# A planner's durations for two engines set to measured ones, with three smaller edits, in a kernel that chains a convolution and two expert layers

## The chip, the cores and the metric

The kernel runs on one core of one Trainium2 chip. The metric is device time in microseconds (us) of one execution, the median over runs. The core's engines are TensorE (PE in the profile; PEld is its weight load), VectorE (DVE), ScalarE (ACT), GpSimd (POOL) and SyncE (SP), which here only issues DMAs. Each engine takes its instructions in the order in which the program lists them and waits at the head of its queue for what an instruction needs.

## The reference

`x` is 2 x 4096 x 192, `weight_gen` 2 x 4096 x 8 x 7, each expert layer has `w_in` 192 x 2048 and `w_out` 2048 x 192, all float32.

```python
w = softmax(weight_gen, over the 7 taps)
y[b, s, h, :] = sum_k w[b, s, h, k] * x_pad[b, s + k, h, :]     # causal, 6 zero rows in front
x1 = y.reshape(8192, 192)
h = relu(x1 @ moe_w_in);   x2 = (h * h) @ moe_w_out              # layer 0
h = x2 @ moe2_w_in;        out = (h * cos(h)) @ moe2_w_out       # layer 1
```

## The kernel before, in words

The 8192 tokens are 16 blocks `b` of 512. A *step* is one block, one layer `m` and one of 16 slices `f` of 128 hidden units; a *phase* is the 16 steps of one block in one layer. The order of phases is written out: layer 0 of blocks 0 to 5 first, then in turn layer 1 of block b - 6 and layer 0 of block b, at the end layer 1 of the last six blocks. There are 32 phases and 512 steps.

Products keep float32's accuracy by splitting: each operand is the sum of a rounded `hi` and a remainder `lo` of the type fp32r. A step has five matmuls (L608) into one of four PSUM buffers `h`, then `between` (L636) makes the activation, and five matmuls (L625 to L631) add it into `acc`. `between` has for layer 0 a Relu on ScalarE (L642) and a square on ScalarE (L646) or VectorE (L648); for layer 1 `kk` on ScalarE (L652), `rr` on VectorE (L655), Abs and Sin on ScalarE (L657, L658) and the product `g` on VectorE (L660). Then come `hi`, a copy on ScalarE (L275), and `lo = g - hi` (L282). In the first six phases `g` lies in PSUM, and `lo` can only be VectorE's. Afterwards `g` is one of two SBUF buffers, and `lo` may go to VectorE or to GpSimd. The inputs of a layer are split in the same way (`xhi`, `xlo`).

The convolution of a block (`attend`, L470) is four products of `x` with the softmax weights on GpSimd (L460), each cut into `PIECES` parts by heads, each followed by a reduction over the taps on VectorE (L475) that frees one of two buffers `pr`. Transposes and a trip through DRAM turn its result into the input of layer 0. The softmax of later blocks has its last part on VectorE (L421 to L428). The weights of both layers are made from the float32 bits by a chain on ScalarE, VectorE and GpSimd (`weight`, L285: L316 to L333, then L275 and L282).

The order of the instructions on every engine comes from a planner, the class `Order` (L58). Each operation is handed to it with `ways`, the engines that may do it and a duration for each, from the formulas `act`, `dve` and `pool` (L175 to L184). `issue` (L119) first gives each operation a due time: TensorE's follow each other by their durations, and an operation that others depend on is due as much earlier as the shortest of its user's durations, a wait of 0.14 us and the operation's own `ahead` make. It then goes forward in planned time. Of the engines an operation may use it takes the one with the earliest end, where `MORE` adds a handicap to an engine's end in this comparison. Operations with `alone` on VectorE or GpSimd also hold a common `port`, so that in planned time they never overlap:

```python
shared = lambda o, e: o.alone and e in ("dve", "pool")
...
    ((max(free.get(e, 0.0), o.at, free.get("port", 0.0) if shared(o, e) else 0.0) + c, e)
     for e, c in o.ways.items()),
    key=lambda v: v[0] + self.MORE.get(v[1], 0.0))
```

Of the operations that can begin first, the one with the earliest due time is issued. On the chip nothing is left of planned times: only the choice of engine and the order on each engine. At the end `take_out` (L687) stores a block's result with four DMAs from `oa` and two from `ob` (L697), all issued by SyncE.

Of the kernel before, what the change touches and what calls it, by code (L numbers as in the profile page):

```python
# [18 lines left out]
P = 128  # L19
# [5 lines left out]
START = 18.0  # L25
LEAD = 6
AHEAD = 2.0
PIECES = 4
ALONE = 8
WARM = 26  # L30

# [10 lines left out]
class Buf:  # L42
    def __init__(self, make, older=None, before=None, tile=None):
        self.make, self.older, self.before, self.tile = make, older, before, tile
        self.log = []
# [12 lines left out]
class Order:  # L58
# [1 line left out]

    SENT, RATE, SEEN = 0.75, 300e3, 0.8

    MORE = {"dve": 0.6, "pool": 0.0, "act": 0.05}
    NEAR = 0.02
    HALF = 0.15
    BEHIND = 4.0

    def __init__(self):
        self.ops, self.tags, self.since = [], {}, 0.0

    def buf(self, pool, shape, dtype, tag, n, name):
        old = self.tags.setdefault(tag, [])
        b = Buf(
            lambda: pool.tile(shape, dtype, tag=tag, bufs=n, name=name),
            old[-n] if len(old) >= n else None, old[-1] if old else None,
        )
        old.append(b)
        return b
# [14 lines left out]
    def op(self, ways, fn, reads=(), writes=(), size=0, behind=None, by=1e9, over=(), since=0.0,  # L93
           alone=True, slack=0.0, ahead=0.0):
        o = Op()
        o.ways, o.fn, o.size = ways, fn, size
        o.alone, o.slack, o.ahead = alone, slack, ahead
        o.late = self.SENT + size / self.RATE + self.SEEN if size else 0.0
        o.behind, o.by, o.since = behind, by, max(since, self.since)
        o.older, o.deps, o.after, o.n = set(over), set(), set(behind or ()), len(self.ops)  # L100
        for write, accesses in ((False, reads), (True, writes)):
            for a in accesses:
                b, key = a if isinstance(a, tuple) else (a, None)
                for p, w, k in b.log:
                    if (w or write) and (k is None or key is None or k == key):
                        o.deps.add(p)
                if b.log:
                    o.after.add(b.log[0][0])
                elif b.before is not None:
                    o.after.add(b.before.log[0][0])  # L110
                if b.older is not None:
                    o.older.add(b.older)
                b.log.append((o, write, key))
        o.deps.discard(o)
        o.after.discard(o)
        self.ops.append(o)
        return o

    def issue(self):  # L119
# [25 lines left out]
        while ready:  # L145
            for o in ready:
                o.end, o.eng = min(
# [3 lines that stand above are left out]
                o.begin = o.end - o.ways[o.eng]  # L151
# [27 lines left out]
def dve(n, fast=False, psum=False):  # L179
    return 0.147 + n / 960 if psum else 0.069 + n / (1600 if fast else 900)  # L180


def pool(n, scalar=False):
    return 0.08 + n * 0.0011 if scalar else 0.155 + n * 0.0017  # L184


@with_exitstack
def conv_moe_kernel(
# [10 lines left out]
    nc = tc.nc  # L199
# [8 lines left out]
    NB = NT // N  # L208
# [15 lines left out]
    dram = ctx.enter_context(tc.tile_pool(name="dram", bufs=1, space=bass.MemoryType.DRAM))  # L224
    order = Order()
    op, buf = order.op, order.buf
    eng = {"act": nc.scalar, "dve": nc.vector, "pool": nc.gpsimd, "sp": nc.sync, "pe": nc.tensor}

    def sbuf(shape, dtype, tag, n, name):
        return buf(sb, shape, dtype, tag, n, name)  # L230
# [4 lines left out]
    def load(dst, out_fn, in_ap, size, key=None, reads=(), by=1e9, queue="sp", behind=None, slack=0.0):  # L235
        op({queue: 0.45}, lambda e: eng[e].dma_start(out=out_fn(), in_=in_ap), reads=reads,
           writes=[(dst, key)], size=size, by=by, behind=behind, slack=slack)
# [47 lines left out]
    def weight(m, part, c0, n):  # L285
        name = f"{part}{m}_{c0}"
        by = -99.0 if m == c0 == 0 and part != "o" else 1e9

        early = dict(queue="act", behind=exps[:1], by=by) if by < 0 else {}
        if m == 0:  # L290
            order.since = 0.0 if by < 0 else 6.5
        stage = lambda tag, n, shape: (
            order.lent(room[tag], tag + "0", f"{tag}{name}") if m == 0 else sbuf(shape, U32, tag, n, f"{tag}{name}"))
        raw = stage("raw", 2, [P, WC, 2])
# [11 lines left out]
        else:  # L306
# [7 lines left out]


        op({"act": act(cols)}, lambda e: nc.scalar.activation(  # L316
            gt().bitcast(F32), top().bitcast(F32), AF.Abs, scale=2.0 ** -112), [raw], [g])

        def lower(e):
            if e == "act":  # L320
                nc.scalar.activation(vt(), low(), AF.Identity, scale=2.0 ** -29)
            else:
                nc.gpsimd.tensor_scalar(
                    out=vt(), in0=low(), scalar1=2.0 ** -29, scalar2=0.0, op0=ALU.mult, op1=ALU.add)
        op({"act": act(cols), "pool": pool(cols, True)}, lower, [raw], [v])
        op({"dve": dve(cols, True)}, lambda e: nc.vector.tensor_scalar(
            out=st(), in0=top(), scalar1=0x80000000, scalar2=None, op0=ALU.bitwise_and), [raw], [sg])
        op({"dve": dve(cols, True), "pool": pool(cols, True)}, lambda e: eng[e].tensor_scalar(
            out=gt().bitcast(F32), in0=gt().bitcast(F32), scalar1=bits(0x0FEFFFFF), scalar2=0.0,
            op0=ALU.min, op1=ALU.max), [], [g])  # L330
# [24 lines left out]
        for i, (bh, hi, bl, lo, src, size) in enumerate(pieces):  # L355
            if part == "b":
# [2 lines left out]
               [sg], [(bh, (f, "hi", i)) for f in fs], over=over)  # L359
            op({"pool": pool(size), "dve": dve(size)}, lambda e, bh=bh, bl=bl, hi=hi, lo=lo, src=src: sub(e, lo(bl.t), src(), hi(bh.t).bitcast(F32)),  # L360
               [sg] + [(bh, (f, "hi", i)) for f in fs], [(bl, (f, "lo", i)) for f in fs], over=over)
        order.since = 0.0

    def weight_order(m):
        cuts = [0] + list(range(2 * P, DFF, WC)) + [DFF]
# [87 lines left out]
    def product(b, i, pr, inner=False, ways=None):  # L453
        step = H if ways else H // PIECES
        for h0 in range(0, H, step):
            hs = slice(h0, h0 + step)

            def go(e, hs=hs):
                t = pr.t.rearrange("p d k -> p k d") if inner else pr.t
                eng[e].tensor_tensor(  # L460
                    out=t.rearrange("p k (h g) -> p k h g", h=H)[:, :, hs],
                    in0=xc[b].t[:, i:i + K, :].rearrange("p k (h g) -> p k h g", h=H)[:, :, hs],
                    in1=wg[b // CB].t[:, b % CB * BS + i, hs].rearrange("p h k -> p k h").unsqueeze(3).to_broadcast(
                        [P, K, step, G]),
                    op=ALU.mult,
                )
            op(ways or {"pool": pool(K * D * step // H)}, go, [xc[b], (wg[b // CB], b % CB)],
               [pr if step == H else (pr, h0)])
# [201 lines left out]
    def sum_halves(s, o1):  # L670
        op({"act": act(N, True)}, lambda e: copy(e, s.t[DB:P], o1.t[DB:P]), [o1], [s])
        op({"dve": dve(N, psum=True)}, lambda e: nc.vector.tensor_tensor(
            out=s.t[0:DB], in0=o1.t[0:DB], in1=s.t[DB:P], op=ALU.add), [o1], [s], alone=False)
# [13 lines left out]
    def take_out(b):  # L687
        o0, o1 = acc.pop((1, b))
        oa = sbuf([P, N], F32, "raw", 2, f"oa{b}")
        ob = sbuf([DB, N], F32, "raw", 2, f"ob{b}")  # L690
        s = sbuf([P, N], F32, "sum", 1, f"os{b}")
        op({"dve": dve(N)}, lambda e: nc.vector.transpose(oa.t, o0.t), [o0], [oa], alone=False)
        sum_halves(s, o1)
        op({"dve": dve(N)}, lambda e: nc.vector.transpose(ob.t, s.t[0:DB]), [s], [ob], alone=False)
        for d0 in range(0, D, 32):
            o, p0 = (oa, d0) if d0 < P else (ob, d0 - P)
            op({"sp": 0.5}, lambda e, o=o, p0=p0, d0=d0: nc.sync.dma_start(  # L697
                out=out[b * N:(b + 1) * N, d0:d0 + 32].rearrange("(j a) d -> a j d", a=32),
                in_=o.t[p0:p0 + 32].rearrange("a (j d) -> a j d", d=32)), [o], [], size=32 * N * 4)

# [6 lines left out]
    for b in range(NB):  # L707
# [10 lines left out]
        if b % CB == 0:  # L718
# [4 lines left out]
            else:  # L723
                n = 14 + 9 * c
# [13 lines left out]
    def late_weight(t, *w):  # L738
        order.since = 2.27 * t + START - 5
        weight(*w)  # L740
        order.since = 0.0

    for t, w in plan:
        if w[0] == 0:
            when(max(math.floor(t), -1), weight, *w)
        else:
            when(math.floor(t), late_weight, t, *w)
# [59 lines left out]
```

## Time and profile before

| | |
|---|---|
| median of 3 runs | 1265.58 us (1265.26 to 1265.69) |
| the profiled execution | 1267.42 us, its span 1265.5 us |
| mean granted TensorE clock | 0.992 |
| busy share of the span | TensorE 96%, ScalarE 84%, GpSimd 71%, VectorE 50% |
| instructions | 16848 |

The span runs from the first to the last instruction of one profiled execution; the few microseconds beside it are the start and end of the program. The busy share of TensorE is modelled from pipelined matmuls. Shares are means over stages with different limits.

### The profile page before, as it was taken

The page shows a single profiled execution, that of the slowest core. Times are in us where ns is not written, and L with a number is a line of the kernel's source. Part 1 is how long each engine was busy: PE and PEld are TensorE (multiplying, and loading weights), DVE is VectorE, ACT ScalarE, POOL GpSimd, SP SyncE. Part 2 cuts the span into 40 slices and gives each one's busy share as a digit, 9 for nine tenths or more (in the row PEclk, how much of TensorE's full clock was granted, in tenths as well). Part 3 has the DMA queues.
Part 4 walks back from the last instruction along what each step waited for, and adds up shares of the span by engine and source line. Part 5 has one row for each costly group of instructions (what it writes and reads, how often), then busy time and mean ns, then how long its engine had stood idle before and what let it go on. Part 6 is the DMA issues. An engine that isn't in the chain of part 4 may idle for free. (4 is left out here: it accounts for less than half of the span.)

```text
span 1265.5 us, 16848 instructions
## 1 busy us (share of the span) xinstructions
PE 1217.9 (96%) x5344; PEld 987.0 (78%) x5344; DVE 636.8 (50%) x916; ACT 1059.9 (84%) x2003; POOL 893.7 (71%) x879
## 2 busy tenths in 40 slices
PE   7999999999999999999999999999999999999997
PEld 6877878788778787787877877778687878888885
DVE  7667777656271453705416163261723315666654
ACT  4888888788796887969779697887978879999996
POOL 3787887938677596876967768687665665666654
PEclk8999999999999999999999999999999999999999
DMA  5405544202212021121201212011110200111001
GB/s 183 125 32 157 153 142 132 78 22 53 57 38 57 21 75 23 40 55 38 72 9 38 57 38 65 9 38 27 45 26 23 49 21 13 30 30 30 13 4 22
DMA packets 90746, 67.81 MB, mean 54 GB/s; under 512 B 55840, under 2 KB 76320, under 8 KB 90656
## 3 DMA queue, kind: packets, MB, share of 16 engines
q1 hardware_dynamic: 90224, 66.21, 19.2%
q8 instruction: 42, 0.69, 0.2%
q10 hardware_dynamic: 432, 0.52, 0.2%
q14 instruction: 48, 0.39, 0.1%
HBM read 47.24 MB, written 19.46 MB: 53 GB/s over the span
## 5 line engine op out<-in xcount | busy, mean ns | idle before, releaser
L282 POOL TENSOR_TENSOR lo<-g,hi 128x512 fp32r<-128x512 f32 x416 | 538.6, 1298 | 296.7 <-ACT hi L275 207.9
L655 DVE SCALAR_TENSOR_TENSOR rr<-kk,h 128x512 f32<-128x512 int32 x256 | 174.0, 683 | 320.9 <-ACT kk L652 319.0
L275 ACT ACTIVATE hi<-g 128x512 fp32r<-128x512 f32 x416 | 259.4, 623 | 5.9 <-DVE g L660 5.3
L660 DVE TENSOR_TENSOR g<-h,rr 128x512 f32<-128x512 f32 x256 | 175.4, 685 | 100.8 <-POOL lo L282 68.4
L626 PE MATMUL acc<-hi,wo 128*128 128x512 f32 x512 | 200.3, 391 | 1.8 <-POOL wo L282 1.8
L625 PE MATMUL acc<-hi,wo 128*128 128x512 f32 x512 | 200.2, 391 | 1.2 <-ACT hi L275 0.7
L630 PE MATMUL acc<-lo,wo 128*128 128x512 f32 x512 | 200.4, 391 | 0.5 <-POOL lo L282 0.4
L627 PE MATMUL acc<-hi,wo 128*128 128x512 f32 x512 | 200.0, 391 | 0.0
L631 PE MATMUL acc<-lo,wo 128*128 128x512 f32 x512 | 200.0, 391 | 0.0
L646 ACT ACTIVATE g<-rr 128x512 f32<-128x512 f32 x160 | 101.2, 633 | 106.3 <-POOL lo L282 104.0
L657 ACT ACTIVATE rr<-rr 128x512 f32<-128x512 f32 x256 | 160.3, 628 | 26.0 <-DVE rr L655 25.4
L642 ACT ACTIVATE rr<-h 128x512 f32<-128x512 f32 x256 | 149.7, 586 | 23.9 <-PE h L608 23.3
L658 ACT ACTIVATE rr<-rr 128x512 f32<-128x512 f32 x256 | 160.8, 630 | 1.8
L460 POOL TENSOR_TENSOR pr<-xc,wgen_late 128x336 f32<-128x336 f32 x192 | 156.0, 871 | 6.8 <-DVE wgen_late L428 5.0
L652 ACT ACTIVATE kk<-h 128x512 int32<-128x512 f32 x256 | 150.5, 588 | 0.9 <-PE h L608 0.7
L626 PEld LDWEIGHTS acc<-hi,wo 128*128 128x128 f32 x512 | 96.4, 188 | 23.1 <-POOL wo L282 2.7
L630 PEld LDWEIGHTS acc<-lo,wo 128*128 128x128 f32 x512 | 96.4, 188 | 22.2 <-POOL lo L282 2.1
L625 PEld LDWEIGHTS acc<-hi,wo 128*128 128x128 f32 x512 | 96.3, 188 | 22.2 <-ACT hi L275 1.1
L631 PEld LDWEIGHTS acc<-lo,wo 128*128 128x128 f32 x512 | 96.5, 188 | 19.9
L627 PEld LDWEIGHTS acc<-hi,wo 128*128 128x128 f32 x512 | 96.5, 188 | 19.9
L475 DVE TENSOR_REDUCE at<-pr 128x192 f32<-128x1344 f32 x56 | 86.5, 1544 | 30.8 <-POOL pr L460 30.3
L282 DVE TENSOR_TENSOR lo<-h,hi 128x512 fp32r<-128x512 f32 x96 | 65.6, 687 | 50.9 <-ACT hi L275 50.2
(547 smaller groups left out, 2180.1 us busy)
## 6 DMA issues: line engine op xcount, KB each, us to landing
xc<-in_x_dram SPq DMA_DIRECT2D x14, 960.0 KB, 6.1
x2d<-x2a SPq DMA_DIRECT2D x16, 256.0 KB, 2.1
x<-x2d SPq DMA_DIRECT2D x32, 128.0 KB, 2.6
x<-x2d SPq DMA_DIRECT2D x16, 256.0 KB, 2.7
out_dram<-oa SPq DMA_DIRECT2D x64, 64.0 KB, 2.0
x1d<-xt SPq DMA_DIRECT2D x56, 64.0 KB, 1.8
x<-x1d SPq DMA_DIRECT2D x14, 256.0 KB, 2.7
x<-x1d SPq DMA_DIRECT2D x28, 128.0 KB, 5.2
```

The lines of the kernel that those rows point to most:

```text
L275: nc.scalar.activation(out, in_, AF.Copy)
L282: eng[e].tensor_tensor(out=out, in0=in0, in1=in1, op=ALU.subtract)
L460: eng[e].tensor_tensor(out=t.rearrange("p k (h g) -> p k h g", h=H)[:, :, hs], in0=xc[b].t[:, i:i + K, :].rearrange("p k (h g) -> p k h g" ...
L625: nc.tensor.matmul(o0.t, lhsT=w(0), rhs=hi.t, start=start, stop=False)
L626: nc.tensor.matmul(o1.t, lhsT=w(2), rhs=hi.t, start=start, stop=False)
L627: nc.tensor.matmul(o0.t, lhsT=w(1), rhs=hi.t, start=False, stop=False)
L630: nc.tensor.matmul(o1.t, lhsT=w(2), rhs=lo.t, start=False, stop=stop)
L631: nc.tensor.matmul(o0.t, lhsT=w(0), rhs=lo.t, start=False, stop=stop)
L655: op({"dve": dve(N, psum=True)}, lambda e: nc.vector.scalar_tensor_tensor(out=r.t, in0=k.t, scalar=-TWO_PI, in1=h.t, op0=ALU.mult, op1=ALU ...
L657: op({"act": act(N)}, lambda e: nc.scalar.activation(r.t, r.t, AF.Abs), [], [r])
L658: op({"act": act(N)}, lambda e: nc.scalar.activation(r.t, r.t, AF.Sin, scale=-1.0, bias=math.pi / 2), [], [r], behind=exps if (b, f) == (0 ...
L660: op({"dve": dve(N, psum=True)}, lambda e: nc.vector.tensor_tensor(out=g.t, in0=h.t, in1=r.t, op=ALU.mult), [h, r], [g], alone=False)
```

## The change

- `PIECES` goes from 4 to 2: a product on GpSimd is two instructions of 672 elements a partition in place of four of 336.
- `pool(n)`, the duration of a GpSimd instruction with two tensors, becomes 0.13 + n * 0.0023 us in place of 0.155 + n * 0.0017; with a scalar its constant is 0.1 in place of 0.08. The handicap of VectorE in the choice of engine goes from 0.6 to 0.4 us.
- `Order` has a default `ahead`, which `weight` sets to 2.0 us for the loads and the chain of the first weights of layer 0 (parts a and b from column 0), so that each of them is due that much earlier.
- The two stores of `ob` of the last block are issued by ScalarE in place of SyncE.

```diff
-PIECES = 4
+PIECES = 2
...
-    MORE = {"dve": 0.6, "pool": 0.0, "act": 0.05}
+    MORE = {"dve": 0.4, "pool": 0.0, "act": 0.05}
...
-        self.ops, self.tags, self.since = [], {}, 0.0
+        self.ops, self.tags, self.since, self.ahead = [], {}, 0.0, 0.0
...
-        o.alone, o.slack, o.ahead = alone, slack, ahead
+        o.alone, o.slack, o.ahead = alone, slack, max(ahead, self.ahead)
...
 def pool(n, scalar=False):
-    return 0.08 + n * 0.0011 if scalar else 0.155 + n * 0.0017
+    return 0.1 + n * 0.0011 if scalar else 0.13 + n * 0.0023
...
         if m == 0:
             order.since = 0.0 if by < 0 else 6.5
+            order.ahead = 2.0 if by < 0 else 0.0
...
-        order.since = 0.0
+        order.since = order.ahead = 0.0
...
-            op({"sp": 0.5}, lambda e, o=o, p0=p0, d0=d0: nc.sync.dma_start(
+
+            queue = "act" if b == NB - 1 and d0 >= P else "sp"
+            op({queue: 0.5}, lambda e, o=o, p0=p0, d0=d0: eng[e].dma_start(
```

## Rows read from the trace of the kernel before

**Rows 1.** Windows: stretch, length, busy (count) of PE, PEld, DVE, ACT, POOL, clock, DMA.

```profile
263.02:335.54 72.52, 72.52 (x322) 60.08 (x320) 39.19 (x50) 60.35 (x112) 51.00 (x47) 1.00 0.18 48
335.54:376.28 40.74, 38.53 (x162) 31.02 (x160) 23.72 (x33) 37.34 (x72) 28.25 (x26) 0.96 0.13 37
376.28:412.78 36.50, 36.50 (x161) 29.96 (x160) 6.91 (x10) 26.59 (x49) 28.59 (x28) 1.00 0.19 49
335.54:1104.20 768.66, 743.00 (x3201) 599.10 (x3200) 319.79 (x444) 645.95 (x1208) 549.08 (x482) 1.00 0.15 38
1104.20:1249.00 144.80, 144.80 (x634) 118.32 (x633) 89.68 (x140) 138.75 (x265) 89.51 (x70) 1.00 0.10 19
```

**Rows 2.** Waits of the whole span: who waited for whom, us, times, longest.

```profile
ACT g L646 <- POOL lo L282: 104.0, 138, 1.3
...
PEld h L608 <- DVE g L660: 46.9, 55, 2.7
```

**Rows 3.** Timeline of GpSimd and ScalarE, end of a layer 0 phase; start, duration.

```profile
409.98 1.29 POOL L282 TENSOR_TENSOR lo<-g,hi 128x512 fp32r<-128x512 f32 x1 [1.32 <-ACT hi L275]
412.59 1.28 POOL L282 TENSOR_TENSOR lo<-g,hi 128x512 fp32r<-128x512 f32 x1 [1.32 <-PE acc L627]
...
411.30 0.63 ACT L646 ACTIVATE g<-rr 128x512 f32<-128x512 f32 x1 [0.97 <-POOL lo L282]
411.84 0.62 ACT L275 ACTIVATE hi<-g 128x512 fp32r<-128x512 f32 x1
```

**Rows 4.** Groups by line, shapes apart; count, busy us, mean ns, idle before.

```profile
L282 POOL TENSOR_TENSOR lo<-g,hi 128x512 fp32r<-128x512 f32 x416 | 538.6, 1298 | 296.7 <-ACT hi L275 207.9 <-PE h L608 27.0 <-PE acc L627 26.6
...
L660 DVE TENSOR_TENSOR g<-h,rr 128x512 f32<-128x512 f32 x256 | 175.4, 685 | 100.8 <-POOL lo L282 68.4 <-ACT rr L658 19.3 <-ACT rr L642 8.8
L655 DVE SCALAR_TENSOR_TENSOR rr<-kk,h 128x512 f32<-128x512 int32 x256 | 174.0, 683 | 320.9 <-ACT kk L652 319.0
L658 ACT ACTIVATE rr<-rr 128x512 f32<-128x512 f32 x256 | 160.8, 630 | 1.8
...
L460 POOL TENSOR_TENSOR pr<-xc,wgen_late 128x336 f32<-128x336 f32 x192 | 156.0, 871 | 6.8 <-DVE wgen_late L428 5.0 <-DVE at L475 1.3 <-PE acc L627 0.5
L652 ACT ACTIVATE kk<-h 128x512 int32<-128x512 f32 x256 | 150.5, 588 | 0.9 <-PE h L608 0.7
...
L282 DVE TENSOR_TENSOR lo<-h,hi 128x512 fp32r<-128x512 f32 x96 | 65.6, 687 | 50.9 <-ACT hi L275 50.2
```

**Rows 5.** Timeline: a VectorE instruction twice, GpSimd beside it (first, last of five).

```profile
82.24 0.20 DVE L425 TENSOR_SCALAR sx<-sx 128x64 f32<-128x64 f32 x1
...
319.90 4.30 DVE L425 TENSOR_SCALAR sx<-sx 128x64 f32<-128x64 f32 x1
...
319.39 1.60 POOL L460 TENSOR_TENSOR pr<-xc,wgen_late 128x336 f32<-128x336 f32 x2
...
322.87 1.29 POOL L282 TENSOR_TENSOR lo<-g,hi 128x512 fp32r<-128x512 f32 x1
```

**Rows 6.** Timeline of the end, and ScalarE's queue issuing three loads at the start.

```profile
1257.17 1.28 POOL L282 TENSOR_TENSOR lo<-g,hi 128x512 fp32r<-128x512 f32 x1 [1.49 <-ACT hi L275]
...
1260.02 1.95 SPq L697 DMA_DIRECT2D out_dram<-oa  x4
1262.07 1.00 SPq L697 DMA_DIRECT2D out_dram<-ob  x2
...
1260.74 0.70 DVE L694 STREAM_TRANSPOSE ob<-os 64x512 f32<-64x512 f32 x1
...
3.69 1.76 ACTq L236 DMA_DIRECT2D wo_early<-in_moe_w_in_dram  x3
```

**Rows 7.** Timeline of the start: the first weights and the first `h` matmul.

```profile
10.96 3.49 POOL L328 TENSOR_SCALAR wiAlo_early<-wiAlo_early 128x256 f32<-128x256 f32 x2 [8.66 <-ACT wiAlo_early L316]
...
22.11 0.75 DVE L331 SCALAR_TENSOR_TENSOR wiB_early<-wiAlo_early,wiB_early 128x256 uint32<-128x256 uint32 x2
...
24.47 0.80 PE L608 MATMUL h<-xlo_(0, 0)_198,wiAhi 128*128 128x512 f32 x1 [3.93 <-ACT wiAhi L275]
```

## The prediction

> **What bounds the kernel now.** I read the windows of the span first, cut where phases begin. Two undisturbed phases, 32 steps of ten matmuls, take 72.52 us [rows 1]: 72.52 / 32 = 2.266 us a step, back to back on TensorE. That is the pace that nothing can beat. From 335.54 to 1104.20 us there are 20 phases, 320 steps, which at that pace need 725.2 us; they take 768.66. So 43.4 us are lost there, nearly all in the nine pairs "phase of layer 1, phase of layer 0": the phase at 335.54 takes 40.74 us against 36.26, the next one 36.50. The four last phases (634 matmuls, 63.4 steps, 143.7 us) lose only 1.1 us of 144.80, 0.28 a phase. The loss goes with the attention's products, which the last phases don't have. TensorE runs at a granted 1.00, which is 2.4 GHz, in most of these windows, so the clock is not the matter.
>
> The waits say how it is lost [rows 2]: TensorE waits for VectorE's `g`, ScalarE's square waits 104.0 us for GpSimd's `lo`. The timeline of the end of a layer 0 phase shows the loop [rows 3]: `lo` starts at 409.98 and the next at 412.59, a cadence of 2.61 us against TensorE's 2.27. With two `g` buffers, square t waits for `lo` t-2. ScalarE's order has that square ahead of the `hi` for which GpSimd's next `lo` waits, so the times add up: `lo` 1.29, square 0.54 to the next issue, `hi` 0.62, and handovers. GpSimd idles 1.32 us in each turn. In the planner's own time this is no loop at all: it costs the subtraction on GpSimd at 0.155 + 512 x 0.0017 = 1.03 us, the trace at 1.298 [rows 4], so that `lo` t-2 counts as done before the square is due. The real engines fall 0.34 us a step behind through a phase, and the next phase, in which ScalarE is busy 37.34 of 40.74 us and can't catch up, pays with TensorE idle.
>
> **The change part by part.** (1) *Durations.* The new formula gives 0.13 + 512 x 0.0023 = 1.308 us for `lo` on GpSimd. The choice of engine turns over too. Before, with both engines idle, GpSimd ended at 1.025 and VectorE counted 0.069 + 512/900 + 0.6 = 1.238, and since both hold the planner's port, VectorE could never win: all 416 of layer 0's and layer 1's subtractions from SBUF stand on GpSimd [rows 4]. After, it is 1.308 against 0.638 + 0.4 = 1.038, and VectorE wins unless it is busy for 0.27 us longer than the port. In a layer 0 phase VectorE is busy 6.91 of 36.50 us [rows 1], so nearly all `lo` go there; in a layer 1 phase 23.72 of 40.74, so perhaps half do. No row shows this subtraction with both inputs in SBUF on VectorE; the nearest is the one from PSUM, 0.687 us [rows 4], and I take that, with 1.298 (no better than GpSimd) as the other end. A pair's 32 `lo` and 4 `xlo` cost 36 x 1.298 = 46.7 us of GpSimd now; on VectorE they would be 36 x 0.687 = 24.7 beside 23.7 + 6.9 busy, 55 of 72.5 us. There is room, and the loop above closes in time: 0.69 + 0.54 + 0.62 = 1.85 us, and with honest durations `hi` would be put first anyway.
>
> What it adds is a wait. VectorE's instructions that share the port with GpSimd stand at the head of an in-order queue, with `rr` and `g` of layer 1 behind them, and ScalarE's Abs and Sin behind those. The trace shows how long such a wait can be [rows 5]: a 0.20 us scale instruction took 4.30 us, until five instructions of GpSimd that stood back to back had ended. GpSimd without a gap doesn't let VectorE in. The Trainium skill (SBUF — State Buffer, Who interferes with whom) has the exclusive port too, for an instruction with two SBUF inputs, but held for one instruction; by that the wait would end with the running one, below the slack worked out next, and the forecast would be some 7 us lower. The row of 4.30 us disagrees, and it decides.
>
> (2) *Two pieces.* Two back-to-back pieces of 336 take 1.60 us now [rows 5], a single one 0.871 [rows 4]; a piece of 672 lies between 1.60 and 1.74, and I take 1.60 (the work in GpSimd is the same, one start fewer). Nothing on the path comes from that; but a run of products, which the two `pr` buffers limit to four pieces of 672, 6.4 us, now has fewer gaps. What hides a stall of VectorE is TensorE's lead: four `h` buffers, 4 x 2.266 = 9.06 us, less the chain that frees one in layer 1, that is 1.13 of matmuls, `kk` 0.588, `rr` 0.683, Abs and Sin 0.63 each, `g` 0.685 and some 0.5 of handovers, 4.85 [rows 4] (Abs taken as Sin). The slack is 4.2 us. A wait of one product (1.6) or two (3.2) costs nothing; a full run of four costs 6.4 - 4.2 = 2.2. In a layer 0 phase the chain is shorter and ScalarE is free for ten us, so I count only the run in the layer 1 half of a pair: between 0 and 2.2 us a pair. As the runs seldom stand without a gap (reductions of `pr` and `lo` that stay on GpSimd break them), I take a third, 0.73.
>
> So after the change the 20 phases lose 9 x (2 x 0.28 + 0.73) + 2 x 0.28 = 12.2 us instead of 43.4: **-31.2**, between -37.8 (no such wait) and -18.0 (each pair pays 2.2).
>
> (3) *First weights ahead.* They only change priorities in the start, where VectorE has no idle time. The first `h` matmul waits until 24.47 for the weights [rows 7]; VectorE's last part of them (L331, two of them in 0.75 us) is at 22.11 behind the split of the first input. Put ahead, it could give at best 24.47 - 22.86 = 1.6 us. At worst VectorE waits in front of its own products for GpSimd's clamp of these weights, two of which took 3.49 us because VectorE's products held the port: half of it, 1.7. Later steps need the same work of VectorE in either order. I take **-0.5**, between -1.6 and +1.7.
>
> (4) *Last stores.* SyncE issues four stores of `oa` from 1260.02 to 1261.97 and the two of `ob` from 1262.07 [rows 6], though `ob` is there at 1261.44. On ScalarE's queue, which is idle by then, they go at about 1261.5. Three issues took 1.76 us there, 0.59 each, against 0.50 on SyncE: the second ends at 1262.7 instead of 1263.07. **-0.4**, between 0 and -0.5. The very last `lo`, 1.28 us on GpSimd with everything waiting for it [rows 6], becomes 0.69 on VectorE: **-0.6**, between 0 and -0.6.
>
> The sum is -31.2 - 0.5 - 0.4 - 0.6 = -32.7 us. The profiled execution took 1267.42 us (span 1265.5): 1234.7. It stood 1.84 above the median of the runs, so beside the median of 1265.58 this is **1232.9, say 1233 us**. The four terms' bounds add up to -40.5 and -16.3, that is 1225 to 1249.
>
> **The rivals.** *VectorE is kept out more than I count.* Each pair pays a full run in both halves, or runs are joined by a `lo` left on GpSimd as in the five of [rows 5]: 4.4 us a pair instead of 0.73 is 9 x 3.7 = 33 us back, the gain is gone. A little over half of that, 18 to 29 us back, gives 1251 to 1262. For it speaks the 4.30 us row; against it that the planner counts the port as exclusive and puts `lo` between products, and that GpSimd pauses where it waits for `hi`.
>
> *Slower: the port puts VectorE on the path.* If ScalarE, with 37.3 of 40.7 us busy in layer 1, can't make up any wait, TensorE's lead is used up by the first and a whole run of 6.4 us counts in each pair: 9 x 6.4 + 5.6 = 63 us lost instead of 43.4, +20, about 1285. It decides from 4.9 us a pair on. The Trainium skill (Perfetto Trace Analysis, Optimizing Scalar/DVE Operations) warns of it: since the two engines share a read port, moving work between them "might not help". The last phases, where no product runs, speak for less harm, and a layer 0 phase, where VectorE has 29 us idle, too.
>
> *`lo` stays on GpSimd.* If VectorE mostly counts as busy, the honest durations alone still mend ScalarE's order. GpSimd is busy 28.25 + 28.59 of 77.2 us in a pair [rows 1], which fits into 72.5; a `lo` behind a product then costs up to 1.3 us a pair: about 1238. By time alone this can't be told from my forecast, but by the counts on L282.
>
> *No change:* the loss is due to something else than this loop, say the transfers around block changes: within 0.2% of 1265.6.
>
> **How the numbers follow.** About 0.2%, 2.5 us, is what a measurement can tell here. Forecast, including the bounds of its terms (1225 to 1249): 0.56. More waits, 1249 to 1262: 0.15. `lo` stays: 0.08. Better than 1225, with waits that end with one instruction of GpSimd: 0.06. No change: 0.05. Slower: 0.10. Faster is 0.56 + 0.15 + 0.08 + 0.06 = 0.85. The range leaves out most of the last two cases and the best end: 1221 to 1262.
>
> **What would show it.** Right: L282 has some 150 to 250 `lo` on VectorE and fewer than 270 on GpSimd; the wait of the square for `lo` falls from 104 us to under 30; a pair takes about 74 us instead of 77.2; VectorE's busy share rises by 10 to 15 points. The price of waits shows as `lo` on VectorE with a mean above 1 us, and as TensorE waiting for `g` behind such a one. Two-piece products show 1.6 us. The first `h` matmul starts between 23 and 26 us. Wrong: `lo` on VectorE takes several us each, layer 1 phases stay above 40 us, or the subtractions' count on VectorE is small.

## The result, and the profile after

The changed kernel takes 1223.28 us (median of 4 runs, 1222.09 to 1224.01) against 1265.59: a ratio of 0.9665, with a 95% interval of 0.9648 to 0.9682. The profiled execution took 1222.77 us with a span of 1220.9. The diff moves the lines from `weight` on down by one to three, so L608 of before is L609 here, L646 is L647, L460 is L461.

The page first: the busy times of the engines, then the groups of the subtraction, of `g` on ScalarE and of the products (count, busy us, mean ns, idle before it).

```profile
PE 1200.1 (98%) x5344; PEld 990.8 (81%) x5344; DVE 842.5 (69%) x1193; ACT 1051.8 (86%) x1994; POOL 569.9 (47%) x499
...
L282 POOL TENSOR_TENSOR lo<-g,hi 128x512 fp32r<-128x512 f32 x204 | 264.8, 1301 | 526.6 <-ACT hi L275 513.2
L282 DVE TENSOR_TENSOR lo<-g,hi 128x512 fp32r<-128x512 f32 x212 | 184.3, 874 | 160.9 <-ACT hi L275 154.1
...
L461 POOL TENSOR_TENSOR pr<-xc,wgen_late 128x672 f32<-128x672 f32 x96 | 156.9, 1703 | 31.6 <-DVE at L476 25.2
...
L647 ACT ACTIVATE g<-rr 128x512 f32<-128x512 f32 x160 | 100.2, 626 | 33.3 <-DVE lo L282 32.0
```

Half of the 416 subtractions went to VectorE, whose busy share rose from 50% to 69%; GpSimd's fell from 71% to 47%. The windows are cut at the same steps as [rows 1] (stretch, length, busy us of PE, PEld, DVE, ACT, POOL with counts, clock, DMA); the last two are the end, and the start from the first `h` up to the seventh phase.

```profile
264.54:337.07 72.53, 72.53 (x321) 60.08 (x320) 49.66 (x69) 64.48 (x120) 34.66 (x27) 1.00 0.18 48
337.07:373.34 36.27, 36.27 (x161) 30.04 (x160) 27.85 (x40) 34.80 (x67) 18.07 (x14) 1.00 0.15 41
373.34:409.80 36.46, 36.46 (x161) 29.95 (x160) 24.00 (x27) 28.81 (x54) 11.03 (x8) 1.00 0.19 49
337.07:1062.60 725.53, 725.53 (x3201) 600.53 (x3200) 491.10 (x661) 644.57 (x1206) 286.59 (x206) 1.00 0.16 40
1062.60:1206.08 143.48, 143.48 (x634) 118.81 (x633) 99.27 (x154) 137.98 (x265) 71.10 (x56) 1.00 0.10 19
1206.08:1220.90 14.82, 8.55 (x38) 6.76 (x36) 5.95 (x9) 5.33 (x10) 2.58 (x2) 0.92 0.18 28
...
24.35:264.54 240.19, 233.11 (x1042) 189.24 (x1043) 179.62 (x273) 190.65 (x379) 164.60 (x192) 0.98 0.37 111
```

The 20 phases that took 768.66 us [rows 1] take 725.53; at 2.266 us a step they need 725.2. So they lost 43.5 us and now lose 0.3. Beside the profile of before, the account of the spans is: up to layer 1's first step 264.54 against 263.02, +1.5; from there to the last step's `h` 941.54 against 985.98, -44.4; the end 14.82 against 16.54, -1.7; in all -44.6. The medians differ by less, 42.3 us, since the profiled execution of before stood 1.84 above its median and this one 0.5 below.

What became of the loop of [rows 3] is seen at the same place, the end of a layer 0 phase, in the timeline of ScalarE and VectorE.

```profile
401.21 0.63 ACT L647 ACTIVATE g<-rr 128x512 f32<-128x512 f32 x1 [0.28 <-DVE lo L282]
401.75 0.61 ACT L275 ACTIVATE hi<-g 128x512 fp32r<-128x512 f32 x1
402.27 0.58 ACT L643 ACTIVATE rr<-h 128x512 f32<-128x512 f32 x1
403.13 0.63 ACT L647 ACTIVATE g<-rr 128x512 f32<-128x512 f32 x1 [0.27 <-DVE lo L282]
...
402.40 0.69 DVE L282 TENSOR_TENSOR lo<-g,hi 128x512 fp32r<-128x512 f32 x1 [1.22 <-ACT hi L275]
404.31 0.69 DVE L282 TENSOR_TENSOR lo<-g,hi 128x512 fp32r<-128x512 f32 x1 [1.22 <-PE h L609]
```

The loop is still there: square waits for `lo`, `lo` for `hi`, `hi` stands behind the square. But `lo` takes 0.69 us, so a turn takes 1.91 (404.31 - 402.40) in place of 2.61, less than TensorE's 2.27. A phase that starts late makes up for it, and TensorE never notices.

### The profile page after: what moved, and what is told of

Same layout as the page of the kernel before. It is cut to its first block, busy times and chain, and to the rows that moved or that the text cites. A ratio compares the mean times of both kernels' runs of the same rounds, so it can differ in the third digit from the quotient of the medians.

```text
span 1220.9 us, 16658 instructions
## 1 busy us (share of the span) xinstructions
PE 1200.1 (98%) x5344; PEld 990.8 (81%) x5344; DVE 842.5 (69%) x1193; ACT 1051.8 (86%) x1994; POOL 569.9 (47%) x499
## 4 chain that ended last, share of the span: by engine, by line
PE 91%; DMA 3%; DVE 2%; ACT 2%; issue 1%; SPq 0%; POOL 0%; DVEq 0%; ACTq 0%
PE h L609 45%; PE acc L628 9%; PE acc L626 9%; PE acc L627 9%; PE acc L632 9%; PE acc L631 9%; PE second L493 1%; DMA xc<-in_x_dram 1%; ACT rr L643 1%; DMA x<-x1d 1%; DMA rawa<-in_moe_w_in_dram 1%; ACT hi L275 0%; ACT h L647 0%; DVE lo L282 0%; DMA exp<-early 0%
## 5 line engine op out<-in xcount | busy, mean ns | idle before, releaser
L282 POOL TENSOR_TENSOR lo<-g,hi 128x512 fp32r<-128x512 f32 x204 | 264.8, 1301 | 526.6 <-ACT hi L275 513.2
L282 DVE TENSOR_TENSOR lo<-g,hi 128x512 fp32r<-128x512 f32 x212 | 184.3, 874 | 160.9 <-ACT hi L275 154.1
L461 POOL TENSOR_TENSOR pr<-xc,wgen_late 128x672 f32<-128x672 f32 x96 | 156.9, 1703 | 31.6 <-DVE at L476 25.2
L647 ACT ACTIVATE g<-rr 128x512 f32<-128x512 f32 x160 | 100.2, 626 | 33.3 <-DVE lo L282 32.0
```

Source lines behind the costliest of these rows:

```text
L282: eng[e].tensor_tensor(out=out, in0=in0, in1=in1, op=ALU.subtract)
```

## The experiments

The time of a single run can differ by some us from one occasion to the next (the kernel before took 1269.42 us beside some of these experiments); so they are compared by the 20 phases of their own profile, cut as above, and by their times where there are several.

**1. Is it the move or the durations?** The changed kernel, with `lo` kept on GpSimd, and `xlo` in the same way:

```diff
-        op({"dve": dve(N, psum=True)} if own else {"dve": dve(N), "pool": pool(N)},
+        op({"dve": dve(N, psum=True)} if own else {"pool": pool(N)},
```

> The changed kernel, but lo and xlo from SBUF may go to GpSimd alone; all durations are the new ones. Theory A (the loss was an order on ScalarE that wrong durations gave, and right durations mend it by themselves): the 20 middle phases lose under 15 us of the 43.4, ScalarE's square waits for lo under 40 us in all, time 1223 to 1240 us. Theory B (the gain comes from taking lo away from GpSimd, whose time is short between products): GpSimd has 416 lo again and the phases still lose 30 us or more, time 1250 to 1266 us.

It took 1223.63 us in its one run. The groups show 416 `lo` on GpSimd again, the windows 20 phases without a loss, and ScalarE's square waits for `lo` 0.4 us in all, in place of 104.0 [rows 2]:

```profile
L282 POOL TENSOR_TENSOR lo<-g,hi 128x512 fp32r<-128x512 f32 x416 | 539.7, 1300 | 247.1 <-ACT hi L275 226.9 <-PE h L609 9.8 <-PE acc L628 6.3
```

```profile
338.17:1063.50 725.33, 725.33 (x3201) 600.80 (x3200) 320.09 (x450) 654.17 (x1206) 547.90 (x421) 1.00 0.15 40
```

GpSimd is as busy as before (547.90 us in these phases; 549.08 in [rows 1]), and nothing is lost. Theory B falls: GpSimd's time was not what was short.

**2. One duration alone.** The kernel before, where the planner counts `lo` at 1.308 us on GpSimd and everything else is as it was. VectorE is taken out of the choice, in which it never won before but would with this number:

```diff
-        op({"dve": dve(N, psum=True)} if own else {"dve": dve(N), "pool": pool(N)},
+        op({"dve": dve(N, psum=True)} if own else {"pool": 1.308},
```

> The kernel before, but the planner counts lo after the first six phases at 1.308 us and on GpSimd alone; every other duration, the handicap, the pieces, the ahead and the stores are those of before. If the order of ScalarE under one wrong duration is the whole loss: the middle loses under 3 us with 416 lo on GpSimd, and the first six phases stay as before: 1219 to 1224 us. If the products' or the weights' durations matter too, 10 us or more stay: 1232 us or above.

1220.68 us (1219.55 to 1223.52), a ratio of 0.9639 (0.9623 to 0.9655). Against what was expected, the first six phases did not stay as they were: in the profile, which is of the slowest of the four runs, they end 2.6 us later (265.59 against 263.02). The windows of the 20 phases, and GpSimd's timeline at the end of a layer 0 phase:

```profile
338.12:1063.45 725.33, 725.33 (x3201) 600.80 (x3200) 337.27 (x447) 653.65 (x1205) 548.38 (x480) 1.00 0.15 40
```

```profile
399.89 1.29 POOL L282 TENSOR_TENSOR lo<-g,hi 128x512 fp32r<-128x512 f32 x1 [0.23 <-ACT hi L275]
402.50 1.29 POOL L282 TENSOR_TENSOR lo<-g,hi 128x512 fp32r<-128x512 f32 x1 [1.32 <-ACT hi L275]
404.42 1.29 POOL L282 TENSOR_TENSOR lo<-g,hi 128x512 fp32r<-128x512 f32 x1 [0.63 <-ACT hi L275]
407.03 1.29 POOL L282 TENSOR_TENSOR lo<-g,hi 128x512 fp32r<-128x512 f32 x1 [1.31 <-ACT hi L275]
```

The cadence alternates, 2.61 and 1.92 us, 2.265 in the mean, which is TensorE's pace. The program's order on ScalarE says why (`sq` is the square, numbered by step, in the layer 0 phase of steps 144 to 159):

```
before:             sq153 hi152 sq154 hi153 sq155 hi154 sq156 hi155 hi156 sq157
as changed:         sq153 hi152 sq154 hi153 sq155 hi154 sq156 hi155 sq157 hi156
lo at 1.308 alone:  hi152 sq153 sq154 hi153 hi154 sq155 sq156 hi155 hi156 sq157
```

Told the true duration, the planner puts every second `hi` ahead of the next square, so that every second turn is short. The changed kernel keeps the bad order and gets by with a shorter `lo`. These are two remedies, and each is enough.

**3. The other two ways to the move.** The kernel before with the new formula for GpSimd alone, with a handicap of 0.3 alone, and with the new handicap of 0.4 alone:

```diff
-    return 0.08 + n * 0.0011 if scalar else 0.155 + n * 0.0017
+    return 0.1 + n * 0.0011 if scalar else 0.13 + n * 0.0023
```

```diff
-    MORE = {"dve": 0.6, "pool": 0.0, "act": 0.05}
+    MORE = {"dve": 0.3, "pool": 0.0, "act": 0.05}
...
+    MORE = {"dve": 0.4, "pool": 0.0, "act": 0.05}
```

> The kernel before with the new formula for pool() alone: handicap 0.6, four pieces, no ahead, stores on SyncE. With 1.308 against 1.238 VectorE is still ahead, by 0.07 us. Theory A and B both expect the middle's loss to go: 1221 to 1232 us, with some 150 to 230 lo on VectorE. A rival C (the handicap or the two pieces carry the gain): 1240 us or more.

> The kernel before with VectorE's handicap at 0.3 and nothing else, so that VectorE wins (0.94 against 1.03 us) while GpSimd keeps its too short durations. Theory A: layer 0 phases are free of the loop, as 0.69 + 0.54 + 0.62 us on VectorE is below 2.27, but layer 1's lo on GpSimd and the products are still planned too short: a part of the loss stays, 5 to 20 us, time 1228 to 1245 us. Theory B: the gain is there in full, 1221 to 1228 us.

> The kernel before with VectorE's handicap at the new 0.4 and the old formula for GpSimd. 0.638 + 0.4 = 1.038 stays behind 1.025, so the subtractions stay on GpSimd with wrong durations and the loop is there: 40 to 46 us lost in the middle, 1260 to 1268 us. If the handicap does something else of weight (squares on VectorE take work from ScalarE), the loss falls: 1250 us or less.

They took 1223.97, 1219.49 and 1268.2 us. All three are single runs. `lo` stands 196, 177 and 0 times on VectorE, and the 20 phases lose 0.1, 0.1 and 43.8 us. The formula alone is the whole gain of the middle, and so is a handicap of 0.3 with all durations wrong: theory A's 5 to 20 us for that were too many. In both, `lo` is short where it is on VectorE, as in the changed kernel. The handicap of 0.4 alone does nothing, since 1.038 stays behind 1.025: by the planner's arithmetic 0.013 us lie between nothing and 43 us. The windows of the last of the three:

```profile
335.91:1104.94 769.03, 742.15 (x3201) 597.38 (x3200) 319.82 (x444) 646.08 (x1208) 549.67 (x482) 1.00 0.15 38
```

**4. A third buffer for the loop.** The kernel before with three `g`:

```diff
-        g = h if own else sbuf([P, N], F32, "g", 2, f"g{t}")
+        g = h if own else sbuf([P, N], F32, "g", 3, f"g{t}")
```

> The kernel before with three buffers g instead of two and nothing else; all 416 lo stay on GpSimd. Theory A (square t waits for lo t-2 with hi t-1 behind it): with a third buffer square t waits for lo t-3, which is done, so GpSimd needs only 1.30 us a step, and the middle loses under 15 us: 1226 to 1238 us. Theory B (GpSimd's time is short): no gain, 1258 to 1267 us.

1238.63 us in its one run; the 20 phases take 744.40 us, so 19.2 are lost in place of 43.5. The buffers are part of the loop, but the third one gives back little more than half, less than theory A expected: the square still waits for `lo` (89.2 us in all against 104.0 [rows 2]). What keeps the other half is not shown.

**5. What VectorE's waits cost.** The changed kernel with products in four pieces and in one, and with three PSUM buffers `h` in place of four (as for the other users of that tag):

```diff
-PIECES = 2
+PIECES = 4
...
+PIECES = 1
```

> The changed kernel with GpSimd's products in four pieces again. Theory D (waits of VectorE for the port are covered by TensorE's lead of four h buffers, whatever the pieces): the middle's 25 phases lose under 2 us as with two pieces, time 1221 to 1226 us; the longest lo on VectorE is under 5.8 us. Theory E (fewer, longer pieces are what lets the planner's order hold): the middle loses 5 us or more, 1228 us or above.

> The changed kernel with each product in one piece of 1344 elements, about 3.3 us by twice the measured 1.70. Theory D: a run of products is still two of them, 6.6 us, as pr has two buffers, so waits of VectorE grow in number but not in length, and the lead covers most of them: the middle loses 0 to 5 us, 1222 to 1229 us. Theory F (a lo that meets a product is the dear case, and its price goes with the piece): 10 us or more are lost in the middle, 1233 us or above.

```diff
-        h = buf(ps, [P, N], F32, "h", 4, f"h{t}")
+        h = buf(ps, [P, N], F32, "h", 3, f"h{t}")
```

> The changed kernel with three PSUM buffers h instead of four. If TensorE's lead is what hides VectorE's waits for the port (slack of 4.2 us with four buffers, 3 x 2.27 - 4.85 = 1.95 us with three), waits above 2 us now show: 25 middle phases lose 10 to 60 us, mostly near products, and layer 1 phases more than layer 0 phases. If something else hides them (lo is needed only steps later), the middle still loses under 3 us: 1220 to 1227 us.

The waits are there. The row of the tile in the changed kernel (minimum, median and maximum in ns) and the timeline of the longest, 5.85 us from 375.32 (its row holds the next `lo` too), beside four instructions of GpSimd without a gap:

```profile
L282 DVE TENSOR_TENSOR lo<-g,hi x212: 641/693/5848, 287.3 to 1212.0; 128x512 fp32r<-128x512 f32 x106
```

```profile
375.32 6.45 DVE L282 TENSOR_TENSOR lo<-g,hi 128x512 fp32r<-128x512 f32 x2 [0.17 <-ACT hi L275]
...
375.22 1.36 POOL L282 TENSOR_TENSOR xlo_(1, 2)_3997<-x,xhi_(1, 2)_3961 128x512 fp32r<-128x512 f32 x1
376.47 4.23 POOL L461 TENSOR_TENSOR pr<-xc,wgen_late 128x672 f32<-128x672 f32 x3
```

That phase, 373.34 to 409.80, is 0.2 us longer than the 36.27 of the one before: the only mark that it left. It is a single event. The run with the stores on SyncE (experiment 6), whose program is the same up to its end, has no `lo` above 1.88 us, and its 20 phases take 725.33:

```profile
L282 DVE TENSOR_TENSOR lo<-g,hi x212: 640/692/1878, 287.4 to 1211.9; 128x512 fp32r<-128x512 f32 x106
```

Most waits are short because they end with the GpSimd instruction that is running. Of the 36 `lo` of the changed kernel that took more than 1 us, 34 ended 0.4 to 0.6 us after the end of the instruction of GpSimd that ran when they began, and behind 20 of these the next product stood without a gap. Here a `lo` of VectorE, from 459.55 to 461.16, ends while GpSimd works on two products back to back, from 459.23 to 462.56:

```profile
459.55 1.61 DVE L282 TENSOR_TENSOR lo<-g,hi 128x512 fp32r<-128x512 f32 x1
...
459.23 3.33 POOL L461 TENSOR_TENSOR pr<-xc,wgen_late 128x672 f32<-128x672 f32 x2
```

The product that `lo` gets ahead of takes 1.9 to 2.0 us in place of 1.5. Only two `lo` waited for more: 3.16 us beside two instructions, and the 5.85 beside four. With four pieces the longest took 1.27 us. With one piece the longest took 3.15 us, eight times, beside a single product of 2.88 in the median, and the 20 phases took 725.34 us, a loss of 0.1:

```profile
L282 DVE TENSOR_TENSOR lo<-g,hi x218: 649/693/3153, 286.6 to 1211.1; 128x512 fp32r<-128x512 f32 x109
```

With three `h`, where no `lo` took above 1.9 us, the kernel took 1237.64 us in its one run, and the 20 phases lose 10.4:

```profile
340.24:1075.88 735.64, 733.41 (x3201) 598.47 (x3200) 503.72 (x667) 643.70 (x1206) 277.48 (x200) 1.00 0.15 39
```

So with four `h` waits of 3 us cost nothing and one of 5.85 almost nothing. That it is TensorE's lead that covers them is likely but not shown: with three `h` the gaps of TensorE in the 20 phases come to 8.9 us, and only 3.3 of them lie within 7 us behind a product on GpSimd, so the greater part is not the price of these waits. The planner also made another order for each of these kernels.

The times are another matter. Four pieces took 1218.98 us (1218.66 to 1219.48; ratio 0.9637, 0.9620 to 0.9653), one piece 1222.44 (1221.86 to 1223.52), on one chip and beside 1222.48 for two pieces with the last stores on SyncE (next experiment). Four are faster by 3.5 us with the same middle (725.33 us): the difference lies before the seventh phase, and theory D's 1221 to 1226 us left it out. The windows of the start with four and with two pieces:

```profile
23.65:261.17 237.52, 231.17 (x1042) 188.56 (x1043) 180.55 (x274) 188.32 (x373) 166.65 (x230) 0.99 0.37 113
```

```profile
24.37:264.63 240.26, 232.48 (x1043) 188.03 (x1044) 179.77 (x273) 190.80 (x379) 164.49 (x192) 0.99 0.37 111
```

2.7 us of difference are in these rows; another 0.7 is the first `h`, which no product on GpSimd precedes and which differs as much among the other profiles. The kernel before with two pieces alone was tried as well:

> The kernel before with products in two pieces and nothing else. From the run of the changed kernel with four pieces, which was 3.4 us faster in the first six phases, two pieces cost 2 to 5 us there; the loop stays as it is: 1266 to 1272 us. If two pieces cost nothing by themselves, 1264 to 1266 us; if fewer, longer products ease GpSimd, below 1263 us.

1272.09 us (1271.58 to 1272.48), a ratio of 1.0048 (1.0033 to 1.0063): slower by 6 us. Between the two profiles the span grows by 4.3 us, 3.6 of them as a longer loss of the 20 phases (772.29 us). By itself this edit is a loss in either kernel. What carries it in the first phases of the changed kernel stays open; from 120 us on, TensorE's weight loads wait there for VectorE's `lo` 4.2 us with two pieces and 1.4 with four.

**6. The two small edits.** The changed kernel without the ahead, and with the last stores on SyncE:

```diff
-            order.ahead = 2.0 if by < 0 else 0.0
+            order.ahead = 0.0
```

```diff
-            queue = "act" if b == NB - 1 and d0 >= P else "sp"
+            queue = "sp"
```

> The changed kernel without the 2.0 us that the first weights are due ahead. If the ahead helps as predicted (0.5 us, at best 1.6), the first six phases end later: 1223 to 1226 us. If the ahead is what made the first six phases longer by 1.5 us (layer 1's first step starts at 264.54 instead of 263.02), they end earlier: 1219 to 1222 us. If the new durations of GpSimd did that, no difference: 1222 to 1224 us.

> The changed kernel with the last two stores on SyncE's queue again. Predicted for the stores: 0.4 us, so 1223.4 to 1224.2 us, with the second store of ob issued 0.3 to 0.5 us later after the end of ob's transpose than in the changed kernel. Rival (SyncE ends no later, since the stores' landing decides): no difference.

1222.31 us (1219.71 to 1223.41) and 1222.48 (1222.27 to 1223.65): neither can be told from the changed kernel. The profile without the ahead has layer 1's first step 1.1 us earlier (263.43 against 264.54), which is less than its four runs differ among themselves. For the stores the end of the two timelines shows what came of them, first as changed, then on SyncE:

```profile
1215.41 1.95 SPq L700 DMA_DIRECT2D out_dram<-oa  x4
...
1216.87 0.93 ACTq L700 DMA_DIRECT2D out_dram<-ob  x2
...
1216.13 0.70 DVE L695 STREAM_TRANSPOSE ob<-os 64x512 f32<-64x512 f32 x1
```

```profile
1215.30 1.95 SPq L700 DMA_DIRECT2D out_dram<-oa  x4
1217.35 1.00 SPq L700 DMA_DIRECT2D out_dram<-ob  x2
...
1216.02 0.70 DVE L695 STREAM_TRANSPOSE ob<-os 64x512 f32<-64x512 f32 x1
```

The issue is over 0.55 us earlier (1217.80 against 1218.35), but from the end of `ob` to the end of the span it is 1220.9 - 1216.83 = 4.07 us on ScalarE's queue and 1220.8 - 1216.72 = 4.08 on SyncE's. The row of DMA activity in the last 5.7 us, in 40 slices of tenths, has the engines at 50% or more from the first store's transfer to the last one's, as changed:

```profile
DMA  0000001788588858897568999996000000000000
```

The DMA engines were at work already when `ob` came. By this row and its like for SyncE the transfers end some 2.5 us after `ob` as changed and 2.7 on SyncE; of the 0.55 us little is left there, and nothing at the end of the span, 1.4 to 1.6 us later. Where the rest goes is not shown. The Trainium skill (DMA: Bandwidth & Descriptors, Issuing engines are not separate DMA queues) has both queues run on the same 16 DMA engines, so that another issuing engine saves the time to issue and no more. The trace agrees: here even that did not shorten the span.

## Why the prediction was right

The forecast was 1233 us in a range of 1221 to 1262; 1223.28 came. It lies below the 1225 to 1249 that got 0.56, in the bracket "better than 1225, with waits that end with one instruction of GpSimd", which got 0.06. The cause and the direction were right; the size of what would stay was not: 0.3 us of loss in the 20 phases, where 12.2 had been reckoned, and 6.6 of these come from one step, the wait of VectorE. Step by step:

- *The loop as the cause of the loss.* Right, by runs that break it in three places: order (experiments 1 and 2), length of `lo` (3), and in part buffers (4).
- *(1) Durations, -31.2.* The mechanism was right, the term was too small: the 20 phases gained 43.1 us. Two parts of what was to stay were mis-sized. The 0.28 us a phase, read from the last phases, was the loop's own remainder and no floor: they take 143.48 us now, nothing above TensorE's pace. And the 0.73 us a pair for VectorE's port were 0. The step carried the 4.30 us of a scale instruction [rows 5] over to `lo`, as if a `lo` too had to wait for a whole run of GpSimd. It didn't: 34 of 36 waits ended with the instruction that was running. The rule that the prediction set aside for the sake of that one row fits `lo`, and the forecast that it gave with it, some 7 us lower, was the better one. The one wait near the 6.4 us of a full run (5.85) cost 0.2. `lo` on VectorE from SBUF takes 0.693 us in the median, as the row from PSUM said (0.687).
- *The closing of the loop.* Forecast 1.85 us, measured 1.91. That true durations would put `hi` first "anyway" was wrong for this kernel: ScalarE still has the square first, and what changed is the engine of `lo`. Where `lo` has no other engine, it is right for every second `hi`.
- *(2) Two pieces, 0.* Wrong: 3.5 us lost, by four pieces in the changed kernel. A piece of 672 takes 1.55 us where all `lo` stay on GpSimd (two pieces alone) and 1.70 in the mean of the changed kernel, where VectorE gets in between (forecast 1.60), but the price arose in the first six phases, for which no term was made.
- *(3) Ahead, -0.5.* Not measurable. The first `h` started at 24.35 against 24.47 [rows 7], but over all profiles it starts between 23.65 and 24.37 with the ahead and between 23.34 and 24.47 without.
- *(4) Stores, -0.4.* Wrong: 0. The issue came earlier as forecast, but the step took for granted that the end of the program follows it. *Last `lo`, -0.6:* the end became 1.7 us shorter, but not because this `lo` did. Before, TensorE waited at its last step, for `hi` and then for `lo`:

```profile
1257.15 0.50 PE L625 MATMUL acc<-hi,wo 128*128 128x512 f32 x1 [0.68 <-ACT hi L275]
...
1258.51 0.51 PE L630 MATMUL acc<-lo,wo 128*128 128x512 f32 x1 [0.40 <-POOL lo L282]
```

  Now `lo` is done at 1212.66, and TensorE runs without a gap until 1214.63. With all `lo` on GpSimd the end is as short, 14.82 us in experiment 1 and 14.77 in experiment 2: what is gone is the lag that the loop left, so the sign was right by luck.
- *The counts.* 212 `lo` on VectorE (150 to 250 forecast), the square's wait for `lo` 32.4 us in place of under 30, a pair 72.7 (74), VectorE's share up by 19 points (10 to 15), `lo` on VectorE 0.874 us in the mean (under 1).
- *The rivals.* `lo` staying on GpSimd was priced at 1238 us; when it was made so, it took 1223.63. VectorE's waits as a loss of their own, and the slower case built on them, were too dear for the same reason as the 0.73; the shared port that speaks against moving work between the two engines cost nothing here. The threshold of that case was also miscounted: by its own sum, 9 x 4.2 + 5.6 = 43.4, it decides from 4.2 us a pair on, not 4.9.

The best version seen is the changed kernel with four pieces, 1218.98 us. The kernel before with one duration changed, and `lo` held on GpSimd, reaches 1220.68; with nothing but the handicap at 0.3 it took 1219.49 in its one run.

## What to carry to other kernels

Where an order is planned ahead, a duration that is wrong by a quarter of a microsecond doesn't cost a quarter: it can put one instruction of an in-order queue ahead of the one that its own release depends on, and then the engines can go round in a loop that is slower than the bound. Look for such a loop where an engine idles in equal gaps beside a queue that waits for it, add up its turn, and compare it with the pace of the bound; then shorten a member or change the order, one of them is enough. Price an edit also in the stage where it isn't meant to act: here the pieces' price in the changed kernel came from the start, not from the middle. And a wait that one row shows for one kind of instruction is not yet the wait of another kind: count how often it comes, and for which.

## What the runs showed of the hardware

How long GpSimd keeps VectorE waiting differs with VectorE's instruction. A scale instruction (L425), 0.17 to 0.20 us long where GpSimd was idle, could wait out a whole run of GpSimd: 4.30 us beside five instructions in [rows 5] and 5.57 beside six later in that trace, in experiment 2 9.46 beside ten, and 8.28 and 8.30 beside nine:

```profile
321.38 9.46 DVE L425 TENSOR_SCALAR sx<-sx 128x64 f32<-128x64 f32 x1
```

It did not always: once, at 250.66 us of the trace of before, it was done after 0.37 us between two instructions of GpSimd.

A subtraction with both inputs in SBUF got in behind the instruction that was running in 34 of 36 cases, though another stood behind it in 20, and that one then took 1.9 to 2.0 us in place of 1.5; two waited for two and for four (3.16 and 5.85 us). The page of the Trainium skill that speaks of the port as held for one instruction (SBUF — State Buffer, Who interferes with whom) agrees with the trace on the exclusion; on when the wait ends it fits nearly all subtractions and not these waits of the scale instruction. Why the two kinds differ, and why two subtractions waited longer, no run here shows.

And the six last stores kept the DMA engines at 50% or more, and with two of them on a second queue the program ended no earlier (4.07 against 4.08 us).
